# Seven block products for two chunks at a time, and float32 numerators for eight more pairs of heads

## The chip, the cores and the metric

The kernel runs on one core of a Trainium2 chip. The core has a matrix engine (TensorE, here PE, with PEld for its weight loads), three engines that work on tiles in on-chip memory (VectorE or DVE, ScalarE or ACT, GpSimd or POOL), and SyncE (SP), which here issues nearly all transfers. PE writes only to PSUM, which has eight banks of 512 float32 values for each of 128 partitions; DVE and ACT read them. The metric is the time of one execution in microseconds (us) on the device; lower is better.

## The reference, cut to what matters

```python
def phi(x):
    proj = np.einsum('bhsd,df->bhsf', x, w_phi)
    proj = proj - np.max(np.abs(proj), axis=-1, keepdims=True)
    return np.concatenate([np.exp(proj), np.exp(-proj)], axis=-1)
q_p, k_p = (phi(q), phi(k))
kv = np.einsum('bhsf,bhsd->bhfd', k_p, v)
num = np.einsum('bhsf,bhfd->bhsd', q_p, kv)
den = np.einsum('bhsf,bhf->bhs', q_p, np.sum(k_p, axis=2))[..., None] + 1e-06
x = (num / den) ...            # 8 batches x 576 tokens = 4608 rows of 8 heads x 64 = 512
g = x @ w_gate                 # 512 -> 1536
silu = g * (1.0 / (1.0 + np.exp(-g)))
return (silu * (x @ w_val) @ w_out)
```

All arrays are float32; the three large weights arrive as float64. A linear attention over 8 batches and 8 heads is followed by a gated feed-forward layer.

## The kernel before, in words

Attention is worked out for one batch and one pair of heads at a time: 32 steps called `attention(i)`, i from 0. The feed-forward layer takes the 4608 tokens in 12 chunks of 384 (c from 0 to 11) and the 1536 hidden columns in 12 tiles of 128 (f from 0 to 11).

Where full float32 precision is wanted at the speed of the faster format (float32r), a value is split into a rounded high part and a remainder, and one product becomes three: high x high, high x low, low x high. `first(c, f)` (L686) makes the *gv* products: 2 banks (gate and value, tiles gv0 and gv1) x 4 pieces of the 512 inputs x 3 terms = 24 products of 128x384. ACT then takes the tanh of half the gate (L716), DVE makes gate x (1 + tanh) (L718) and multiplies with the value (L721). `parts` (L737) splits that: cast hh on ACT (L741), remainder hl on DVE (L742). `second(c, f)` (L747) adds it through the third weight into three *o* banks: 3 x 3 products of 128x512. At f = 11 ACT copies each o bank to one of two osb buffers (L782), and SP stores it (L785). `put_off` holds a `second` back until the next tile's `first` is queued, so that PE has 24 gv products to do while hh and hl are made.

Chunks 0 to 2 have their gv products first, tile by tile as the weights are unpacked; the hidden values of chunks 1 and 2 go to memory (`keep`, `fetch`, h_dram) and their `second` comes later. From chunk 3 on, `first` and `second` alternate, and the low parts of the weights are loaded again from wlo_dram for each tile (`low_parts`, L683): 512 KB for gv and 256 KB for o.

Attention up to i = 7 (the "early" pairs of heads) uses plain float32 products. From i = 8 on all is split: keys ks (L378, L380), queries qs (L519, L521), the features qh and ql (L579, L582), the sums kvh and kvl (L456, L460); the numerators are 4 groups of 6 products work<-qh/ql,kvh/kvl. The result num / den is divided on DVE (L616 to L620) and split into xh and xl (L632, L634), the gv operands, which have room for three chunks.

The order on each engine is not written by hand: `Plan` takes steps with assumed costs, dependences and a rank, plays them through and issues them in the order it finds, with manual scheduling. Feed-forward steps outside PE have the lowest rank number and go first; on PE attention goes first and feed-forward products fill up. So every engine, SP with its transfers too, has one fixed line of work. All PE products but a few stand at line 282, in the helper `matmuls`.

Of the kernel before, what the change touches and what calls it, by code (L numbers as in the profile page):

```python
# [17 lines left out]
P = 128  # L18
# [23 lines left out]
EARLY_PAIRS = 8  # L42

# [3 lines left out]

# [11 lines left out]
class Plan:  # L59
# [3 lines left out]
    LAG = {"PE": 220, "ACT": 90, "DVE": 90, "SP": 2000}  # L63
# [24 lines left out]
    def run(self):  # L88
# [11 lines left out]
        def start(e):  # L100
# [33 lines left out]
            for t in s.then:  # L134
                n += 1
                heapq.heappush(events, (freed if t.eng == e and e in ("ACT", "DVE", "PE") else done, n, "dep", t))
# [29 lines left out]
def dve(n):  # L166
    return 150 + 1.04 * n
# [5 lines left out]

def act(n):
    return 190 + 0.86 * n
# [11 lines left out]
def favor_attention_moe(ctx: ExitStack, tc: tile.TileContext, qT, kT, v, w_phi, wg, wv, wo, out):  # L187
# [7 lines left out]
    h_dram = tc.dram_tile([EARLY, NFT, P, CH], F32, name="h_dram")  # L195

# [139 lines left out]
    x_ready = {}  # L336
# [4 lines left out]
    def attention(i, rank):  # L341
        b, pr = divmod(i, NPAIR)
        plan.early = early = i < EARLY_PAIRS
        split = not early
        j = i % 2 if early else 1
        vec = nc.vector
# [108 lines left out]
        for ones in range(2):  # L455
            kvc.append(add("ACT", act(4 * D), lambda ones=ones: nc.scalar.copy(  # L456
                cut(kv_high() if split else kvs[j], ones), sums(ones)), [kv_steps[-1], *(use("kvs") if i != EARLY_PAIRS else first_late("kvs"))], rank))
# [112 lines left out]
        done = [[f1], [f1]]  # L570
# [16 lines left out]
        for h in range(2):  # L587
            for part in range(2):
# [4 lines left out]
                def numerators(key=key, h=h, c=c):  # L593
                    o = work[plan.bank[key]][:, :SH]
                    terms = []
                    for k in range(2):
# [4 lines left out]
                        else:  # L601
                            terms.append((kvs[j][:, n], (qe, qx)[k][j][:, h, c]))
# [3 lines left out]
                free = last.get(("num", i - 1))  # L606
                copied.append(add("ACT", act(SH), lambda key=key, ra=ra, c=c: nc.scalar.copy(  # L607
                    num[ra, c], work[plan.bank[key]][ra, :SH]), [nu, free], rank))
                copied.append(add("ACT", act(SH), lambda key=key, ra=ra, rb=rb, c=c: nc.scalar.activation(  # L609
                    den[ra, c], work[plan.bank[key]][rb, :SH], AF.Copy, bias=1e-6), [nu, free], rank, give=key))  # L610
# [17 lines left out]
            [(base, 0, 0, CH), (base + 1, 0, CH, CH // 2)]  # L628
        for c, at, start, width in cuts:
            src = num[:, start:start + width]  # L630
# [8 lines left out]
        last["num", i] = lo  # L639
# [86 lines left out]
    def keep(c, f, j, made):  # L726

        th_free[j] = h_kept[c, f] = add("SP", P * CH * 4, lambda: nc.sync.dma_start(h_dram[c, f], th[j]), [made], FIRST)

    def fetch(c, f):  # L730
        j = ffn["th"] % TH_SETS
        ffn["th"] += 1
        return j, add("SP", P * CH * 4, lambda: nc.sync.dma_start(th[j], h_dram[c, f]), [h_kept[c, f], th_free[j]], FIRST)
# [13 lines left out]
    def second(c, f, hidden, low):  # L747
        b, ready = hidden
        readers, lo, lo_ready = low
        for t in range(NT):  # L750
            sl = slice(t * P, (t + 1) * P)

            def go(t=t, sl=sl):
                if t == 0:
# [4 lines left out]
                    ((hh[b][:, sl], w2_hi[f]), (hh[b][:, sl], lo), (hl[b][:, sl], w2_hi[f])))])  # L759
# [3 lines left out]
            if f == NFT - 1:  # L763
                if n_out[0] == NCH * NT - 1:
# [126 lines left out]
```

## Time and profile before

| | us |
|---|---|
| median of 3 runs | 1269.33 (1268.94 to 1270.84) |
| the profiled execution, first to last instruction | 1273.1 |
| PE busy | 1262.2 |
| DVE busy | 876.4 |
| ACT busy | 651.5 |
| POOL busy | 1.3 |
| transfers | 168 MB, 132 GB/s on average |

The page gives busy times, the span in 40 slices, the chain of work that ended last, groups of instructions and transfers. A group's row has line, engine, operation, what it writes and reads, shapes and count, then busy us and mean ns, then idle time before it and who ended it. A matmul's shown duration reaches into the next one; what one costs in a row of them is read from the distance of their starts.

### The profile page before, as it was taken

The page shows a single profiled execution, that of the slowest core. Times are in us where ns is not written, and L with a number is a line of the kernel's source. Part 1 is how long each engine was busy: PE and PEld are TensorE (multiplying, and loading weights), DVE is VectorE, ACT ScalarE, POOL GpSimd, SP SyncE. Part 2 cuts the span into 40 slices and gives each one's busy share as a digit, 9 for nine tenths or more (in the row PEclk, how much of TensorE's full clock was granted, in tenths as well). Part 3 has the DMA queues.
Part 4 walks back from the last instruction along what each step waited for, and adds up shares of the span by engine and source line. Part 5 has one row for each costly group of instructions (what it writes and reads, how often), then busy time and mean ns, then how long its engine had stood idle before and what let it go on. Part 6 is the DMA issues. An engine that isn't in the chain of part 4 may idle for free.

```text
span 1273.1 us, 19796 instructions
## 1 busy us (share of the span) xinstructions
PE 1262.2 (99%) x7427; PEld 1189.9 (93%) x7427; DVE 876.4 (69%) x1674; ACT 651.5 (51%) x1383; POOL 1.3 (0%) x13
## 2 busy tenths in 40 slices
PE   9999999999999999999999999999999999999998
PEld 8887999999889999999999999999999999999998
DVE  6998999998887778762788888822488886222222
ACT  5787433336676666632765666611466665121211
POOL 0000000000000000000000000000000000000000
PEclk8999999999999999999999999999999999999999
DMA  4543455555564344444433444354444342444443
GB/s 120 144 119 102 140 174 175 174 165 167 159 204 123 112 117 113 148 123 127 129 104 113 129 124 120 105 161 129 125 120 119 105 132 84 124 149 125 149 126 106
DMA packets 112111, 168.15 MB, mean 132 GB/s; under 512 B 52752, under 2 KB 59408, under 8 KB 112016
## 3 DMA queue, kind: packets, MB, share of 16 engines
q1 hardware_dynamic: 111552, 166.64, 44.1%
q8 instruction: 58, 0.95, 0.3%
q14 instruction: 37, 0.30, 0.1%
q10 hardware_dynamic: 464, 0.26, 0.1%
HBM read 143.26 MB, written 23.59 MB: 131 GB/s over the span
## 4 chain that ended last, share of the span: by engine, by line
PE 92%; DVE 4%; DMA 1%; ACT 1%; SPq 1%; issue 0%; DVEq 0%; ACTq 0%
PE gv L282 46%; PE o L282 25%; PE work L282 12%; PE kv L435 8%; PE kv L428 1%; DMA out_dram<-osb 0%; PE o L502 0%; DVE km L410 0%; DVE kp L415 0%; DMA shared<-in_wg_dram 0%; DMA shared<-in_wo_dram 0%; DVE qy L491 0%; DMA wbd<-in_w_phi_dram 0%; DVE km L486 0%; ACT den L609 0%
## 5 line engine op out<-in xcount | busy, mean ns | idle before, releaser
L282 PE MATMUL gv<-xh,w_hi 128*128 128x384 f32 x1152 | 388.6, 337 | 0.8 <-DVE th L718 0.8
L282 PE MATMUL gv<-xh,w_lo 128*128 128x384 f32 x1152 | 386.9, 336 | 0.0
L282 PE MATMUL gv<-xl,w_hi 128*128 128x384 f32 x1152 | 386.1, 335 | 0.0
L282 PEld LDWEIGHTS gv<-xh,w_hi 128*128 128x128 f32 x1152 | 216.4, 188 | 5.7 <-DVE th L718 1.1
L282 PEld LDWEIGHTS gv<-xl,w_hi 128*128 128x128 f32 x1152 | 216.5, 188 | 4.6
L282 PEld LDWEIGHTS gv<-xh,w_lo 128*128 128x128 f32 x1152 | 216.1, 188 | 0.0
L716 ACT ACTIVATE th<-gv 128x384 f32<-128x384 f32 x144 | 70.9, 492 | 263.9 <-PE gv L282 263.1
L718 DVE SCALAR_TENSOR_TENSOR th<-th,gv 128x384 f32<-128x384 f32 x144 | 79.2, 550 | 149.6 <-ACT th L716 147.7
L282 PE MATMUL o<-w_hi,hl 128*128 128x512 f32 x432 | 171.5, 397 | 0.2 <-DVE hl L742 0.2
L282 PE MATMUL o<-w_hi,hh 128*128 128x512 f32 x432 | 170.9, 396 | 0.3 <-ACT osb L782 0.3
L282 PE MATMUL o<-w_lo,hh 128*128 128x512 f32 x432 | 170.3, 394 | 0.0
L741 ACT CAST hh<-th 128x384 fp32r<-128x384 f32 x144 | 73.6, 511 | 164.3 <-DVE th L721 148.1
L721 DVE TENSOR_TENSOR th<-th,gv 128x384 f32<-128x384 f32 x144 | 79.4, 552 | 71.1 <-PE gv L282 68.7
L435 PEld LDWEIGHTS kv<-vf,kp 128*128 128x128 f32 x1024 | 123.2, 194 | 3.1 <-ACT kp L419 1.3
L435 PE MATMUL kv<-vf,kp 128*128 128x66 f32 x1024 | 123.2, 274 | 1.3 <-ACT kp L419 1.0
L742 DVE TENSOR_TENSOR hl<-th,hh 128x384 fp32r<-128x384 f32 x144 | 79.5, 552 | 32.8 <-ACT hh L741 32.1
L282 PEld LDWEIGHTS o<-w_hi,hl 128*128 128x128 f32 x432 | 81.4, 188 | 19.4 <-DVE hl L742 0.6
L282 PEld LDWEIGHTS o<-w_hi,hh 128*128 128x128 f32 x432 | 81.7, 189 | 12.7 <-ACT osb L782 0.8
L282 PEld LDWEIGHTS o<-w_lo,hh 128*128 128x128 f32 x432 | 81.4, 188 | 12.2
L616 DVE STREAM_TRANSPOSE qe<-den 128x576 f32<-128x576 f32 x32 | 24.9, 778 | 92.0 <-ACT den L609 92.0
L607 ACT COPY num<-work 64x288 f32<-64x288 f32 x102 | 40.2, 394 | 51.2 <-PE work L282 49.8
L282 PE MATMUL work<-qh,kvh 128*128 128x288 f32 x192 | 60.8, 317 | 0.3 <-DVE kp L415 0.3
(124 smaller groups left out, 1871.1 us busy)
## 6 DMA issues: line engine op xcount, KB each, us to landing
w_lo<-wlo_dram SPq DMA_DIRECT2D x108, 512.0 KB, 3.6
w_lo<-wlo_dram SPq DMA_DIRECT2D x132, 256.0 KB, 3.0
wlo_dram<-w_lo SPq DMA_DIRECT2D x36, 256.0 KB, 2.3
out_dram<-osb SPq DMA_DIRECT2D x35, 256.0 KB, 3.3
kin<-in_kT_dram SPq DMA_DIRECT2D x32, 256.0 KB, 2.9
vf<-in_v_dram SPq DMA_DIRECT2D x64, 128.0 KB, 2.7
qin<-in_qT_dram SPq DMA_DIRECT2D x24, 288.0 KB, 2.9
shared<-in_wg_dram SPq DMA_DIRECT2D x12, 512.0 KB, 3.6
```

Of the source, the lines that this page charges most:

```text
L282: nc.tensor.matmul(o, l, r, start=a, stop=z)
L428: nc.tensor.matmul(ps_kv[:, 2 * k * D2:2 * (k + 1) * D2], room[:, 0, k], vf[j][:, 4].rearrange("p h d -> p (h d)"), start=False, stop=k == 1)
L435: nc.tensor.matmul(o, room[:, 2 * (t - t0) + h, k], vf[j][:, t, h], start=t + h + k == 0, stop=False)
L607: copied.append(add("ACT", act(SH), lambda key=key, ra=ra, c=c: nc.scalar.copy(num[ra, c], work[plan.bank[key]][ra, :SH]), [nu, free], rank))
L616: t0 = add("DVE", dve(S), lambda: vec.transpose(turned, den), [*copied, *done[0], *done[1]], rank)
L716: s1 = add("ACT", act(CH), lambda: nc.scalar.activation(t_, ps_gv[0][:, :CH], AF.Tanh, scale=0.5), [ends[0], th_free[j]], FIRST)
L718: s2 = add("DVE", dve(CH), lambda: nc.vector.scalar_tensor_tensor(out=t_, in0=t_, scalar=1.0, in1=ps_gv[0][:, :CH], op0=ALU.add, op1=ALU.m ...
L721: s3 = add("DVE", dve(CH), lambda: nc.vector.tensor_tensor(out=t_, in0=t_, in1=ps_gv[1][:, :CH], op=ALU.mult), [s2, ends[1]], FIRST)
L741: s4 = add("ACT", act(CH), lambda: nc.scalar.copy(hh[b], th[j]), [made, hid_free[b]], FIRST)
L742: s5 = add("DVE", dve(CH), lambda: nc.vector.tensor_tensor(out=hl[b], in0=th[j], in1=hh[b], op=ALU.subtract), [s4], FIRST)
```

## The change

**Feed-forward, chunks 4 to 11.** They are taken as four pairs of chunks. With the 512 inputs cut in two halves, and gate and value as the two columns of a 2 x 2 block product, two chunks by two halves times two halves by (gate, value) needs 8 block products; the change uses the scheme with 7 products and 15 sums (Strassen's, in Winograd's form). Each of the 7 blocks is 2 pieces x 3 terms = 6 gv products of 128x384, so a tile has 42 for two chunks where it had 48. The sums of the tokens (s1, s2 and two more) are made in `operands` on DVE, from x that attention now stores in x_dram (`held`), and all seven operands are split on ACT and DVE. The sums of the weights are made once, by `mixed`, on POOL, 12 additions of 128x256 for each tile, and stored in wt_dram; `load_ring` streams them back through six buffers that held the gv weights. The sums of the results are made in the banks and through copies: gv0 (gv_145 below) collects four blocks, and ACT copies its state three times on the way; gv1 (gv_146) has two sums of its own, and DVE joins them with the copies. The `second` of the job before is cut into its three thirds, which stand between the blocks. The hidden values of chunk c+1 go to memory, and its twelve `second` follow when the pair's twelve tiles are done.

**Chunks 1 to 3.** `mixed` is queued while chunk 2's second products, chunk 3's first and chunk 3's second are due. Chunk 3's hidden values go to memory too.

**Attention, i = 8 to 15.** Keys and queries stay split, the numerators do not: 4 groups of 2 float32 products (kvs, qe, qx), without L579, L582 and L460.

```diff
+SPLIT_FROM = 16
+PAIRS = 4
+RING = 6
-        split = not early
+        split = i >= SPLIT_FROM
+        held = [(start, width) for c, at, start, width in cuts if c >= PAIRS]
+        if held:
+            x_stored[b, pr] = add("SP", P * width * 4, lambda start=start, width=width, token=token: nc.sync.dma_start(
+                x_dram[pr, :, token:token + width], num[:, start:start + width]), [t3], rank)
-    def second(c, f, hidden, low):
+    def second(c, f, hidden, low, parts_of=range(NT)):
-        for t in range(NT):
+        for t in parts_of:
...
+    def mixed(f, rank):
+        get = add("SP", P * 4 * DM * 2, lambda: nc.sync.dma_start(src.bitcast(F32), wlo_dram[f, :, :2 * DM]),
+                  [lo_stored[f, 0], lo_stored[f, 1], *old[0], *x_free[1]], rank)
...
+        g0 = add("POOL", 4 * pool2(2 * P), whole, [get, *old[1], *x_free[2]], rank)
+        g1 = add("POOL", 4 * pool2(2 * P), combine, [g0, *old[2]], rank)
+        g2 = add("ACT", act(8 * P), lambda: nc.scalar.copy(high, sums()), [g1, *old[3]], rank)
+        g3 = add("POOL", 4 * pool2(2 * P), rest_of, [g2], rank)
...
+    def load_ring(m, n):
+        k = m % RING
+        after, ring_user[k] = ring_user[k], []
+        return add("SP", P * 8 * P * 4, lambda: nc.sync.dma_start(
+            flat(w1_hi[k]).bitcast(F32), wt_dram[:, 2 * n:2 * n + 2].rearrange("p n h c -> p (n h c)")),
+            [*after, *w_spread[2 * n // 7], *w_spread[(2 * n + 1) // 7]], FIRST)
+    def operands(c):
...
+        l0 = split(0, a11, [got[0]])
+        l1 = split(1, a12, [got[1]])
+        d1 = combine(s1, a21, a22, ALU.add, [got[2], got[3], *temp_free[0]])
+        d2 = combine(s2, s1, a11, ALU.subtract, [d1, got[0], *temp_free[1]])
+        l2 = split(2, s2, [d2])
+        d3 = combine(a21, a11, a21, ALU.subtract, [d1, got[0]])
+        l3 = split(3, a21, [d3])
+        l4 = split(4, s1, [d1])
+        l5 = split(5, a22, [got[3]])
+        d4 = combine(a12, a12, s2, ALU.subtract, [l1, d2])
+        l6 = split(6, a12, [d4])
...
+    def pair(c, base):
...
+            part = lambda t: second(*job, range(t, t + 1)) if job else None
+            p1 = mult(0, bank_b, True, False, b_read)
+            y1 = copy(0, p1)
+            p2 = mult(1, bank_c, True, True, c_read)
+            g1 = joined(0, [p2, y1])
+            ja, ga = gate(snap[0], [g1])
+            p6 = mult(2, bank_b, False, False, [y1])
+            y2 = copy(1, p6)
+            part(0)
+            p7 = mult(3, bank_b, False, False, [y2])
+            y3 = copy(2, p7)
+            p5 = mult(4, bank_c, True, False, [g1])
+            v2 = joined(2, [p5, y3])
+            p4 = mult(5, bank_b, False, True, [y3])
+            jb, gb = gate(lambda: bank_b[:, :CH], [p4])
+            part(1)
+            p3 = mult(6, bank_c, False, True, [v2])
+            v1 = joined(1, [p3, y2])
+            part(2)
+            b_read[:], c_read[:] = [gb], [v1]
+            ha = valued(ja, 1, [ga, v1])
+            hb = valued(jb, 2, [gb, v2])
+            keep(c + 1, f, jb, hb)
+            put_off(c, f, parts(ja, ha), low2(f))
...
+        for f in range(NFT):
+            put_off(c + 1, f, parts(*fetch(c + 1, f)), low2(f))
+    for n in range((NCH - PAIRS) // 2):
+        pair(PAIRS + 2 * n, 7 * NFT // 2 * n)
```

What the plan makes of it, at three places. First, PE at the end of a pair's last tile (chunks 6 and 7): the last block ends in gv_146, o_144 takes the third third of tile 10's job, and o_142 and o_143 begin tile 11's (operands hh_133 and hl_135). Now:

```order
L1030 MATMUL gv_146<-w_hi_78,w_hi_76 128x384
L1030 MATMUL gv_146<-w_hi_77,w_hi_76 128x384
L290 MATMUL o_144<-w_hi_93,hh_132 128x512
L290 MATMUL o_144<-w_lo_1367,hh_132 128x512
L290 MATMUL o_144<-w_hi_93,hl_134 128x512
L290 MATMUL o_142<-w_hi_94,hh_133 128x512
L290 MATMUL o_142<-w_lo_1496,hh_133 128x512
L290 MATMUL o_142<-w_hi_94,hl_135 128x512
L290 MATMUL o_143<-w_hi_94,hh_133 128x512
```

Before, PE at the end of chunk 10's last tile: 24 gv products, then the o products of the tile before (weight w_hi_91), whose operands were made meanwhile.

```order
L282 MATMUL gv_144<-xh_98,w_lo_94 128x384
L282 MATMUL gv_144<-xh_98,w_hi_80 128x384
L282 MATMUL gv_144<-xl_101,w_hi_80 128x384
L282 MATMUL gv_144<-xh_98,w_lo_94 128x384
L282 MATMUL o_140<-w_hi_91,hh_130 128x512
L282 MATMUL o_140<-w_lo_95,hh_130 128x512
L282 MATMUL o_140<-w_hi_91,hl_132 128x512
```

Tile 11's o products now come three o products after the gv products that they depend on; before, a tile's came behind the next tile's 24 gv products.

Second, DVE at the same turn (part_4961 and part_5135 are the buffers of s1 and s2, and of the copies out of the banks; the row at L1042 joins bank and copy, L1055 multiplies with the gate, hl_135 is tile 11's remainder, hl_134 that of chunk 7's first job, L985 and L989 make the next pair's operands). Now:

```order
L1055 TENSOR_TENSOR th_131<-th_131,part_5135 128x384
L989 TENSOR_TENSOR xl_104<-part_4724,op_hi 128x768
L1042 TENSOR_TENSOR part_4961<-gv_146,part_4961 128x384
L1055 TENSOR_TENSOR th_130<-th_130,part_4961 128x384
L762 TENSOR_TENSOR hl_134<-th_128,hh_132 128x384
L985 TENSOR_TENSOR part_4961<-part_4722,part_4724 128x768
L762 TENSOR_TENSOR hl_135<-th_130,hh_133 128x384
```

Before, DVE's rows for two tiles of chunk 11:

```order
L718 SCALAR_TENSOR_TENSOR th_127<-th_127,gv_143 128x384
L721 TENSOR_TENSOR th_127<-th_127,gv_144 128x384
L742 TENSOR_TENSOR hl_133<-th_127,hh_131 128x384
L718 SCALAR_TENSOR_TENSOR th_128<-th_128,gv_143 128x384
L721 TENSOR_TENSOR th_128<-th_128,gv_144 128x384
L742 TENSOR_TENSOR hl_132<-th_128,hh_130 128x384
```

Between the last gv product and hl, DVE had one multiplication; now it has a join and a multiplication that belong to the job, and three rows that do not.

Third, ACT in one tile of the last two pairs of chunks (gv_145 is copied at L1038; part_4961 also holds the gate's sum, of which L1049 takes the tanh). Now:

```order
L1038 COPY part_4961<-gv_145 128x384
L1049 ACTIVATE th_128<-part_4961 128x384
L1038 COPY part_4961<-gv_145 128x384
L1038 COPY part_5135<-gv_145 128x384
L1049 ACTIVATE th_129<-gv_145 128x384
L761 CAST hh_132<-th_128 128x384
```

Before, ACT in three tiles of chunk 11:

```order
L716 ACTIVATE th_128<-gv_143 128x384
L741 CAST hh_130<-th_128 128x384
L716 ACTIVATE th_129<-gv_143 128x384
L741 CAST hh_131<-th_129 128x384
L716 ACTIVATE th_126<-gv_143 128x384
```

Three copies have come in for two chunks' tile, and the second of them stands behind the first tanh.

More of the change, by code (lines that the diff above doesn't have):

```diff
@@ L59 @@
 class Plan:
-    LAG = {"PE": 220, "ACT": 90, "DVE": 90, "SP": 2000}
+    LAG = {"PE": 220, "ACT": 90, "DVE": 90, "POOL": 200, "SP": 2000}
     BYTES = 250.0
@@ L135, in start @@
                 n += 1
-                heapq.heappush(events, (freed if t.eng == e and e in ("ACT", "DVE", "PE") else done, n, "dep", t))
+                heapq.heappush(events, (freed if t.eng == e and e in ("ACT", "DVE", "PE", "POOL") else done, n, "dep", t))
             if s.give is not None:
@@ L456, in attention @@
             kvc.append(add("ACT", act(4 * D), lambda ones=ones: nc.scalar.copy(
[L457 removed]
+                cut(kv_high() if split else kvs[kj], ones), sums(ones)),
+                [kv_steps[-1], *use("kvs"), *first_late("kvs")], rank))
         if split:
@@ L567, in attention @@
                 qx[j][:, h], qx[j][:, h], AF.Exp, scale=-1.0)))]
-        done = [[f1], [f1]]
+        done = [[f1], [f1]] if early else [[f1[h]] for h in range(2)]
         if split:
@@ L788, in second, with copy @@
-        hid_free[b] = done
-        readers.append(done)
+            if t == NT - 1:
+                hid_free[b] = done
+                readers.append(done)
+            if f < NFT - 1:
+                continue
+            if n_out[0] == NCH * NT - 1:
+                halves = [pool.tile([P, DM // 2], F32, name=f"osb_last{k}", tag=tag) for k, tag in enumerate(("num", "den"))]
+                for k, eng in enumerate(("ACT", "DVE")):
+                    cols = slice(k * DM // 2, (k + 1) * DM // 2)
+                    rows = out[c * CH + t * P:c * CH + (t + 1) * P, cols]
+                    def copy(k=k, cols=cols, t=t, o=halves[k]):
+                        if k:
+                            nc.vector.tensor_scalar(out=o, in0=ps_o[t][:, cols], scalar1=0.5, scalar2=None, op0=ALU.mult)
+                        else:
+                            nc.scalar.activation(o, ps_o[t][:, cols], AF.Copy, scale=0.5)
+                    cp = add(eng, act(DM // 2), copy, [done], FIRST)
+                    q = nc.sync if k else nc.scalar
+                    add("SP" if k else "ACT", P * DM * 2 if k else 60, lambda q=q, rows=rows, o=halves[k]: q.dma_start(rows, o), [cp], FIRST)
+                continue
@@ new lines, in favor_attention_moe, with wide_tile @@
+    wide = {}
+    def wide_tile(name, tag, shape=(P, 8 * P), dtype=F32):
+        if name not in wide:
+            wide[name] = pool.tile(list(shape), dtype, name=name, tag=tag)
+        return wide[name]
+    for f in range(NFT):
+        mixed(f, FIRST)
+    for f in range(NFT):
+        put_off(2, f, parts(*fetch(2, f)), low_parts_at_rest(f, NFT + f))
+    attend((EARLY + 1) * CH)
+    w_used = {}
+    for f in range(NFT):
+        j, h = first(EARLY, f, low_parts(f, 0))
+        w_used[f] = ffn["pe"]
+        keep(EARLY, f, j, h)
+        put_off()
```

203 lines of the change are left out of this document (166 added, 37 removed).

## The prediction

> **What bounds the kernel now.** I read the page's part 1 first, then the 40 slices and the chain that ended last, then the windows, then the chain piece by piece.
>
> ```profile
> PE 1262.2 (99%) x7427; PEld 1189.9 (93%) x7427; DVE 876.4 (69%) x1674; ACT 651.5 (51%) x1383; POOL 1.3 (0%) x13
> DVE  6998999998887778762788888822488886222222
> PE 92%; DVE 4%; DMA 1%; ACT 1%; SPq 1%; issue 0%; DVEq 0%; ACTq 0%
> PE gv L282 46%; PE o L282 25%; PE work L282 12%; PE kv L435 8%; PE kv L428 1%; DMA out_dram<-osb 0%; PE o L502 0%; DVE km L410 0%; DVE kp L415 0%; DMA shared<-in_wg_dram 0%; DMA shared<-in_wo_dram 0%; DVE qy L491 0%; DMA wbd<-in_w_phi_dram 0%; DVE km L486 0%; ACT den L609 0%
> ```
>
> TensorE (PE) carries 92% of the chain, and almost half of it is gv, the first products of the feed-forward part. A busy PE in this profile is not yet a PE without gaps, so the rate is read from the chain's pieces late in the run, and the other engines' load from windows (columns: stretch, its length, then busy us and instructions of PE, PEld, DVE, ACT, POOL, then clock, DMA share, GB/s).
>
> ```profile
> 1153.74 4.19 PE gv L282 x24
> 1157.93 2.09 PE o L282 x9
> 1160.02 4.19 PE gv L282 x24
> ...
> 200.00:300.00 100.00, 100.00 (x567) 97.15 (x566) 93.89 (x178) 41.53 (x75) 0.00 (x0) 1.00 0.51 166
> 291.00:530.00 239.00, 238.03 (x1446) 221.37 (x1445) 190.05 (x363) 160.61 (x343) 0.00 (x0) 0.99 0.48 141
> 1150.00:1200.00 50.00, 50.00 (x265) 46.84 (x264) 13.34 (x24) 8.91 (x19) 0.00 (x0) 1.00 0.44 127
> ```
>
> The pieces touch: 24 gv products take 4.19 us (0.1746 us each), nine o products 2.09 us (0.232 us each), and nothing lies between. DVE reached 94% at 200 to 300 us with PE still full. So **time is PE work**, and a change pays what it takes from PE, less every gap it opens.
>
> **Removed: products.** Chunks 4 to 11 had 8 x 288 = 2304 gv products; four pairs of chunks at 7 blocks x 12 tiles x 6 have 2016. 288 x 0.1746 = **-50.3 us**. Their weights now come as 512 KB pieces from wt_dram; the o products are the same in number.
>
> **Added: float32 numerators.** Pairs of heads 9 to 16 use 8 float32 products each in place of 24 split ones.
>
> ```profile
> 24.24 0.65 PE L282 MATMUL work<-qe,kvs 128*128 128x288 f32 x2
> ...
> 26.18 1.90 PE L435 MATMUL kv<-vf,kp 128*128 128x66 f32 x16
> ...
> 301.56 0.38 PE L282 MATMUL work<-qh,kvh 128*128 128x288 f32 x1
> ...
> 303.24 0.61 PE L428 MATMUL kv<-vf,kp 128*128 128x132 f32 x4
> ...
> L582 DVE TENSOR_TENSOR ql<-qx,qh 128x576 fp32r<-128x576 f32 x48 | 36.2, 754 | 0.0
> L460 DVE TENSOR_TENSOR kvl<-kv,kvh 128x256 fp32r<-128x256 f32 x48 | 18.7, 417 | 0.0
> ```
>
> Four float32 products (each shown as two) fill 24.24 to 26.18: 0.485 us each. Twelve split ones fill 301.56 to 303.24: 0.14 each. A pair of heads costs 8 x 0.485 - 24 x 0.14 = +0.52 us, eight of them **+4.2 us** on PE. DVE sheds four L582 and two L460 per pair of heads, 3.85 us, 31 in all; that is worth nothing by itself while PE covers it.
>
> **Added: handoffs inside a pair's loop.** Bank gv_145 is copied out by ACT while PE goes on adding to it, so PE waits for copies. The measured handoffs:
>
> ```profile
> 1180.63 0.33 PE L282 MATMUL gv<-xh,w_lo 128*128 128x384 f32 x1
> 1180.81 0.33 PE L282 MATMUL gv<-xh,w_hi 128*128 128x384 f32 x1
> 1181.00 0.49 ACT L716 ACTIVATE th<-gv 128x384 f32<-128x384 f32 x1 [3.04 <-PE gv L282]
> 1181.53 0.55 DVE L718 SCALAR_TENSOR_TENSOR th<-th,gv 128x384 f32<-128x384 f32 x1 [2.98 <-ACT th L716]
> 1183.09 0.56 DVE L721 TENSOR_TENSOR th<-th,gv 128x384 f32<-128x384 f32 x1 [1.00 <-PE gv L282]
> 1183.73 0.51 ACT L741 CAST hh<-th 128x384 fp32r<-128x384 f32 x1 [2.23 <-DVE th L721]
> 1184.28 0.56 DVE L742 TENSOR_TENSOR hl<-th,hh 128x384 fp32r<-128x384 f32 x1 [0.64 <-ACT hh L741]
> ```
>
> ACT starts 0.19 us after PE goes on to the next product, DVE about 0.20; DVE to ACT takes 0.08, ACT to DVE 0.04. The second copy stands on ACT behind a tanh. From the end e of the second block: join on DVE e+0.20 to 0.75, tanh e+0.83 to 1.32, copy to 1.81, PE free to go at about e+1.86 (0.05 for the way back, as from ACT's end at 1203.58 to PE's start at 1203.63 in the rows of the next part). PE has a block (1.05) and a third of an o job (0.70) until e+1.75. The stall is 0.11 us, in 24 loops with nothing else to run and 24 that attention both fills and delays: about 0.12 x 48 = **+6 us** (0 if the copy of 384 columns is faster than the tanh; 15 if attention's ACT work of 0.68 us pieces gets in front each second time).
>
> **Added: the turn between the two chunks of a pair.** The order puts the last job of chunk c and the first of c+1 side by side.
>
> ```profile
> L380 DVE TENSOR_TENSOR ks<-kin,ks 128x640 fp32r<-128x640 f32 x24 | 19.7, 822 | 4.7 <-ACT ks L378 3.8 <-DMA qin<-in_qT_dram 0.7
> out_dram<-osb SPq DMA_DIRECT2D x35, 256.0 KB, 3.3
> 1202.98 0.60 ACT L782 ACTIVATE osb<-o 128x512 f32<-128x512 f32 x1 [2.64 <-DMA out_dram<-osb]
> 1203.63 0.50 PE L282 MATMUL o<-w_hi,hh 128*128 128x512 f32 x1 [0.35 <-ACT osb L782]
> 319.60:323.00 3.40, 2.58 (x14) 1.81 (x12) 3.37 (x6) 3.40 (x8) 0.00 (x0) 1.00 0.65 208
> 323.00:326.40 3.40, 3.25 (x11) 2.43 (x11) 3.17 (x6) 2.80 (x6) 0.00 (x0) 0.64 0.39 119
> ```
>
> First gap: the last job's operand needs join, product, cast, remainder after the last block: 0.20 + 0.55 + 0.03 + 0.55 + 0.08 + 0.51 + 0.04 + 0.55 + 0.05 = 2.56 us, and only 0.70 us of o work covers it. Before, 24 gv products lay in front. At the second and third turn the order also pushes other work in on DVE: ahead of the join a 768-wide remainder (0.96, from L380's 822 at 640 wide and 754 at 576, of which 0.8 delays), behind the product hl of the next chunk (0.55) and a 768-wide sum (0.96), the cast running beside them: 2.56 - 0.70 + 0.8 + 0.55 + 0.96 - 0.6 = 3.6. Turn by turn: 0.8 (attention fills 1.5 after the same sum), 3.6, 3.6, 1.9; together 9.9 us. Second gap: the third copy out of o needs an osb buffer, which is free when the first one's store has landed: 0.20 + 0.60 + 3.3 + 0.60 + 0.05 = 4.75 us after the first third; PE has four thirds, 2.8 us. 1.95 us, four times: 7.8. Together **+18 us**, and **+2 us** for the clock: after PE had idled 0.8 of 3.4 us (the row at 319.60) it was granted 0.64 of the clock on average for 3.4 us, which would cost up to 1.7 us a turn, but the second gap absorbs most.
>
> **Added: mixing the weights on POOL.** 144 additions of 128 x 256, two inputs, while chunks 1 to 3 are worked on.
>
> ```profile
> masks.py:199 POOL TENSOR_SCALAR_AFFINE_SELECT ident<-ident 128x128 f32<-128x128 f32 x1 | 0.3, 288 | 0.0
> L881 POOL MEMSET const-bfloat16-1.0<- 128x1 bf16 x1 | 0.1, 111 | 0.0
> L616 DVE STREAM_TRANSPOSE qe<-den 128x576 f32<-128x576 f32 x8 | 6.2, 777 | 25.3 <-ACT den L609 25.3
> ```
>
> No row shows such an addition. POOL's one-input pass over 128 columns took 288 ns, an empty instruction 111: 1.4 ns a column and input. 256 columns: 0.47 us with one input (low end), 0.83 with two (taken), 1.66 (twice that, high end). A tile has 12 of them, a cast of about 1.1 us and handoffs: 12 us at 0.83. PE's work from the end of chunk 2's first products to the first pair is 288 x 0.1746 + 321 x 0.232 + eleven or twelve pairs of heads at some 9 us (work, kv: 21% of the span over 32 pairs is 8.4, and 0.5 for float32), near 229 us, 19 us a tile. Hidden, up to 1.4 us an addition; at 1.66 it is 22 us a tile, 36 us late. ACT and SP take these steps in line, so what is late there holds the evacuation of PE's banks and the loads behind.
>
> DVE is the closer limit there. It did 190 us in 291 to 530 us with eight pairs of heads (L616 in that window). Now: 190 - 29 for the dropped splits + 45 for three more pairs at some 15 + 10 for the first operands = 216 of 229, 94%, what it managed at 200 to 300. I take **+5 us** for this stage, with 0 and 48 as bounds (48: POOL's 120 us hold DVE up for two fifths of their time).
>
> The Trainium skill's "SBUF — State Buffer", under "Who interferes with whom", says that a VectorE instruction with two SBUF inputs and a GpSimd instruction that reads SBUF exclude each other for a whole instruction. Nothing here could show it (POOL worked 1.3 us). By it the forecast would be the second rival below, without it the first.
>
> **Sum**: -50.3 + 4.2 + 6 + 18 + 2 + 5 = -15.1 us. The profiled execution spans 1273.1 us, 0.3% above the 1269.33 median of the runs; the difference is carried over: **1254 us**.
>
> **Rivals.**
> 1. *The turns are filled and DVE keeps pace.* Then -50.3 + 4.2 + 6 = -40, 1229 us. For it: PE never waited long before, and the dropped splits take away the idles at 320 us. Against: the order shows no other PE work at three turns. Chance 0.17 (1222 to 1238).
> 2. *POOL and DVE hold each other up while the weights are mixed; slower than before.* PE's products of attention wait for DVE. DVE at 94% has no room: each microsecond that POOL holds it beyond some 5 comes out at the end. A third of POOL's 120 us is 40, 35 beyond that room: 1254 - 5 + 35 = 1284 us. The gain is gone once 20 us are lost in that stage. Against it: DVE's reads of PSUM and its transposes and reductions, over half of its work, have one SBUF input or none. Chance 0.16.
> 3. *The weight stream becomes the bound.* A loop moves 3.5 x 512 + 256 + 192 = 2240 KB, 2.29 MB, in 9.5 us: 241 GB/s, twice the present rate.
>
> ```profile
> GB/s 120 144 119 102 140 174 175 174 165 167 159 204 123 112 117 113 148 123 127 129 104 113 129 124 120 105 161 129 125 120 119 105 132 84 124 149 125 149 126 106
> 355.00:360.00 5.00, 5.00 (x42) 4.87 (x40) 0.42 (x2) 4.32 (x11) 0.00 (x0) 1.00 0.80 254
> ```
>
> 254 GB/s was reached for 5 us at a share of 0.80, so it should fit, with six buffers of 2.7 us each ahead. Were 204 (the best slice) the limit, a loop would take 11.2 us: +1.7 x 24 = 41, 1295 us. Chance 0.08.
> 4. *Balance*: a store that lands 3 us later (landing times vary with what is queued ahead) and half a clock at each turn bring 1254 + 4 x 4 = 1270. Chance 0.06.
>
> **How the numbers follow.** Forecast (1238 to 1266.8): 0.53. A measurement of this kernel tells about 0.2% from no change, 1266.8 to 1271.9. Faster: 0.53 + 0.17 = 0.70; same 0.06; slower 0.16 + 0.08 = 0.24. The range that should hold 8 in 10 goes from 1226, inside the first rival, to 1288, inside the second.
>
> **What would show it.** gv products: 3168 at 0.175 us apart. Numerators: qe,kvs and qx,kvs 128 records each. Turns: idle of PE before o with DVE hl, then ACT osb as releaser, four times 1 to 4 us and 2 us, and a granted clock below 1 there. Loop: some 0.1 us before the third block with the copy on ACT as releaser. Mixing: POOL's addition near 0.83 us, DVE's two-input rows no longer than before (754, 552), and no PE idle from 314 to 550 us. Wrong, if PE idles there in tens of us, if DVE's means grow by a tenth or more while POOL runs, or if DMA is named as releaser of gv.

## The result, and the profile after

The changed kernel takes 1305.07 us (median of 4 runs, 1301.61 to 1308.66), the kernel before, run beside it, 1270.07. The ratio is 1.0272, 95% interval 1.025 to 1.0294: **slower by 35 us**, where 15 us faster was forecast. The profiled execution spans 1306.9 us.

These are the page's part 1, the slices of TensorE, POOL and the clock, and the chain that ended last, for the changed kernel:

```profile
PE 1251.3 (96%) x7076; PEld 1146.7 (88%) x7076; DVE 969.8 (74%) x1770; ACT 717.5 (55%) x1491; POOL 121.4 (9%) x157
PE   9999999999999889889999999999999999899998
POOL 0000000004443323540000000000000000000000
PEclk9999999999999988889999999999999999899999
PE 79%; DVE 12%; ACT 4%; DMA 2%; issue 2%; SPq 0%; DVEq 0%; ACTq 0%
```

351 matmul records have gone, 11 us of busy time with them, and the span has grown all the same: PE is no longer full. Most of its dips and of those of its clock lie in slices 14 to 18 (some 425 to 590 us), in the second half of POOL's work. The chain, 92% PE before, now leaves PE for 21% of the span, and DVE has most of that.

The windows tell the two stages apart (columns: stretch, its length, then busy us and instructions of PE, PEld, DVE, ACT, POOL, then clock, DMA share, GB/s). First the changed kernel: the mixing stage, the stage behind it, and 100 us of the last pair's loops.

```profile
310.00:600.00 290.00, 259.88 (x1454) 230.83 (x1453) 222.24 (x377) 185.17 (x382) 117.27 (x142) 0.94 0.77 243
600.00:760.00 160.00, 159.88 (x990) 152.52 (x988) 137.87 (x259) 107.33 (x225) 0.00 (x0) 1.00 0.68 219
1160.00:1260.00 100.00, 100.00 (x534) 93.08 (x533) 45.72 (x82) 31.65 (x66) 0.00 (x0) 1.00 0.75 244
```

PE idles 30.1 of the 290 us in which the weights are mixed, and its granted clock there is 0.94, another 0.06 x 290 = 17 us. In the stage behind, and in the loops of the pairs at 244 GB/s, it is full. Who PE waits for (instruction, releaser, total us, times, longest): the first three rows are of the mixing stage alone, the other three of the whole run.

```profile
PE work L290 <- DVE kp L424: 15.4, 7, 5.1
PE o L290 <- DVE hl L762: 6.0, 5, 1.6
PE work L290 <- ACT qe L574: 4.3, 1, 4.3
...
PE o L290 <- ACT osb L806: 9.6, 5, 2.9
PE o L290 <- DVE hl L762: 7.3, 8, 1.6
PE o L290 <- ACT hh L761: 5.5, 4, 1.8
```

While the weights are mixed, PE waits above all for attention's pieces on DVE, and 6.0 of the 7.3 us for hl belong to this stage too. Behind it, from 600 us on, PE waits 9.5 us for osb, 4.6 for hh and 1.2 for hl: these 15.3 us are the turns. The loops of the last pair, in the chain's pieces, show what a loop costs when nothing else runs:

```profile
1199.41 3.32 PE gv L1030 x18
1202.73 0.70 PE o L290 x3
1203.43 1.04 PE gv L1030 x6
1204.47 0.70 PE o L290 x3
1205.17 3.12 PE gv L1030 x18
1208.29 0.70 PE o L290 x3
1208.99 3.30 PE gv L1030 x18
```

One loop is 1208.99 - 1199.41 = 9.58 us; its 42 gv and 9 o products without a gap are 42 x 0.1746 + 9 x 0.232 = 9.42. The 0.16 us over lie in the first stretch of 18, which takes 3.32 us where the other takes 3.12. So products cost what was forecast, and a loop's handoffs 0.16 us.

One turn, 1122 to 1134 us, as the timeline has it (start, duration, in brackets the idle time before and its releaser):

```profile
1123.94 0.56 DVE L1055 TENSOR_TENSOR th<-th,part 128x384 f32<-128x384 f32 x1
1124.53 0.51 ACT L761 CAST hh<-th 128x384 fp32r<-128x384 f32 x1 [0.85 <-DVE th L1055]
1125.10 0.50 PE L290 MATMUL o<-w_hi,hh 128*128 128x512 f32 x1 [1.78 <-ACT hh L761]
...
1131.90 0.60 ACT L806 ACTIVATE osb<-o 128x512 f32<-128x512 f32 x1 [2.06 <-DMA out_dram<-osb]
...
1132.55 0.79 PE L290 MATMUL o<-w_hi,hh 128*128 128x512 f32 x1 [2.82 <-ACT osb L806]
1133.14 0.63 PE L290 MATMUL o<-w_lo,hh 128*128 128x512 f32 x1
...
1133.57 0.63 PE L290 MATMUL o<-w_hi,hl 128*128 128x512 f32 x1
...
1134.00 0.63 PE L290 MATMUL o<-w_hi,hh 128*128 128x512 f32 x1
```

Both gaps that the prediction described are there, 1.78 us for the gate's chain and 2.82 us for the third eviction's store. Behind the second the o products start 0.43 us apart, in place of 0.232, until 1138.69 us: the granted clock from 1132.5 to 1136 us is 0.50. That costs 2.9 us more.

### The profile page after: what moved, and what is told of

It is laid out like the page before. It is cut to its first block, busy times and chain, and to the rows that moved or that the text cites. A ratio compares the mean times of both kernels' runs of the same rounds, so it can differ in the third digit from the quotient of the medians.

```text
span 1306.9 us, 20317 instructions
## 1 busy us (share of the span) xinstructions
PE 1251.3 (96%) x7076; PEld 1146.7 (88%) x7076; DVE 969.8 (74%) x1770; ACT 717.5 (55%) x1491; POOL 121.4 (9%) x157
## 4 chain that ended last, share of the span: by engine, by line
PE 79%; DVE 12%; ACT 4%; DMA 2%; issue 2%; SPq 0%; DVEq 0%; ACTq 0%
PE gv L1030 25%; PE o L290 21%; PE gv L290 13%; PE work L290 11%; PE kv L444 7%; DMA out_dram<-osb 1%; PE kv L437 1%; DVE qx L572 1%; DVE qm L557 1%; DVE qe L569 1%; DVE hl L762 1%; DVE km L419 1%; DVE qe L549 1%; DVE kp L424 1%; ACT qe L574 1%
## 5 line engine op out<-in xcount | busy, mean ns | idle before, releaser
L1030 PE MATMUL gv<-xh,w_hi 128*128 128x384 f32 x768 | 217.5, 342 | 0.4
L290 PE MATMUL o<-w_hi,hh 128*128 128x512 f32 x432 | 177.2, 410 | 15.3 <-ACT osb L806 9.6
L290 PE MATMUL o<-w_hi,hl 128*128 128x512 f32 x432 | 175.0, 405 | 7.3 <-DVE hl L762 7.3
L290 PE MATMUL o<-w_lo,hh 128*128 128x512 f32 x432 | 173.8, 402 | 0.0
L761 ACT CAST hh<-th 128x384 fp32r<-128x384 f32 x144 | 73.6, 511 | 141.1 <-DVE th L1055 64.6
L1042 DVE TENSOR_TENSOR part<-gv,part 128x384 f32<-128x384 f32 x144 | 80.0, 555 | 82.4 <-PE gv L1030 77.7
L290 PE MATMUL gv<-xh,w_hi 128*128 128x384 f32 x384 | 132.8, 346 | 1.0 <-DVE th L738 1.0
L290 PE MATMUL gv<-xl,w_hi 128*128 128x384 f32 x384 | 130.3, 339 | 0.0
L290 PE MATMUL gv<-xh,w_lo 128*128 128x384 f32 x384 | 130.3, 339 | 0.0
L1030 PE MATMUL gv<-xl,w_hi 128*128 128x384 f32 x384 | 128.6, 335 | 0.0
L290 PEld LDWEIGHTS o<-w_hi,hh 128*128 128x128 f32 x432 | 83.5, 193 | 30.1 <-ACT osb L806 12.7
L1038 ACT COPY part<-gv 128x384 f32<-128x384 f32 x144 | 68.5, 475 | 74.7 <-PE gv L1030 71.2
L1030 PE MATMUL gv<-op_hi,w_hi 128*128 128x384 f32 x384 | 106.8, 335 | 0.0
L290 PEld LDWEIGHTS gv<-xh,w_hi 128*128 128x128 f32 x384 | 73.6, 192 | 2.2 <-DVE th L738 1.4
L290 PEld LDWEIGHTS gv<-xl,w_hi 128*128 128x128 f32 x384 | 73.5, 191 | 0.8
```

The source lines that it names most:

```text
L290: nc.tensor.matmul(o, l, r, start=a, stop=z)
L761: s4 = add("ACT", act(CH), lambda: nc.scalar.copy(hh[b], th[j]), [made, hid_free[b]], FIRST)
L1030: nc.tensor.matmul(o[:, :CH], l, r, start=begin and i == 0, stop=i == len(terms) - 1, skip_group_check=True)
L1038: s = add("ACT", act(CH), lambda: act_.copy(snap[n](), bank_b[:, :CH]), [after, *snap_free[n]], FIRST)
L1042: return add("DVE", dve(CH), lambda: vec.tensor_tensor(out=snap[n](), in0=bank_c[:, :CH], in1=snap[n](), op=ALU.add), after, FIRST)
```

## The experiments

All times are medians, each beside the kernel before on the same chip (1270.07 us beside the changed kernel, 1271 to 1273 beside the others). In short:

| run | us | ratio to before (95%) |
|---|---|---|
| changed kernel | 1305.07 | 1.0272 (1.025 to 1.0294) |
| e1 no additions on POOL | 1297.85 | 1.0194 (1.0171 to 1.0216) |
| e2 additions that nobody waits for | 1315.74 | 1.0342 (1.0314 to 1.0369) |
| e3 stores of mixed weights left out | 1309.65 | 1.029 (1.0263 to 1.0317) |
| e4 kernel before, float32 numerators | 1277.87 | 1.0042 (1.0026 to 1.0058) |
| e5 planner's rate 350 | 1295.17 | 1.0177 (1.0162 to 1.0193) |
| e6 kernel before, rate 350 | 1278.73 | 1.0051 (1.0035 to 1.0066) |
| e7 turns mended | 1290.82 | 1.0147 (1.0123 to 1.0172) |
| e8 e5 and e7 | 1275.74 | 1.0025 (1.0014 to 1.0036) |
| e9 rate 350 from 250 us on | 1287.53 | 1.0119 (1.01 to 1.0137) |
| e10 e9 and e7 | 1269.91 | 0.9979 (0.9966 to 0.9991) |
| e11 e10 without additions | 1262.25 | 0.9918 (0.9895 to 0.9941) |
| e12 e10, rate 400, stores of chunks 0 to 3 on ScalarE's queue | 1284.3 | 1.0091 (1.007 to 1.0113) |
| e13 e10 with 300 | 1271.48 | 1.0001 (0.9978 to 1.0024) |
| e14 e10 with 450 | 1288.0 | 1.0122 (1.0103 to 1.014) |
| e15 e10 with 600 | 1313.22 | 1.0315 (1.0285 to 1.0345) |
| e16 e10, the same stores on ScalarE's queue | 1287.32 | 1.0108 (1.0066 to 1.0151) |

### POOL, the bytes, and the numerators (e1 to e4)

The first theory was rival 2 of the prediction: POOL's additions hold DVE up. Its rivals: what waits for POOL's results is late; the mixing's bytes fill the wire.

e1 makes none of the three groups of additions (the first is shown); ScalarE's copy and one store take other data of the same size:

```diff
-        g0 = add("POOL", 4 * pool2(2 * P), whole, [get, *old[1], *x_free[2]], rank)
+        g0 = add("POOL", 4 * pool2(2 * P), lambda: None, [get, *old[1], *x_free[2]], rank)
...
-        g2 = add("ACT", act(8 * P), lambda: nc.scalar.copy(high, sums()), [g1, *old[3]], rank)
+        g2 = add("ACT", act(8 * P), lambda: nc.scalar.copy(high, hi[:, :8 * P]), [g1, *old[3]], rank)
```

> The changed kernel with POOL's 144 additions left out; ScalarE's copy takes the high part of the weights in place of the sums, and the store that took the sums' low part takes that copy, so that the bytes moved and the order on every other queue stay as they were. The sums of weights are not computed. If POOL's additions (by the hold-up of VectorE or by the waits on their results) cost what the stage from 300 to 600 us lost, some 30 us of idle TensorE and 16 us of lower clock, then about 1250 to 1262 us, and VectorE's qs L531 falls from a mean of 945 ns there back to about 754. If the DMA bytes or the attention that is squeezed into this stage cost it, 1298 to 1306 us.

e2, the same, with three groups of additions on tiles that nothing else reads:

```diff
+        def alone():
...
+            for n in range(4):
+                gp.tensor_tensor(out=sums()[:, block(n)], in0=full()[:, block(n)], in1=full()[:, block((n + 1) % 4)], op=ALU.add)
...
+        g0 = add("POOL", 4 * pool2(2 * P), alone, [get, *old[1], *x_free[2]], rank)
```

> As the run without additions, but POOL makes 144 additions of two SBUF operands of the same size on two tiles that nothing else reads, started by the same loads. The sums of weights are not computed. If the additions cost time because they hold up VectorE (rival 2 of the prediction), it is nearly as slow as the changed kernel: 1295 to 1308 us, with qs L531 above 900 ns while POOL runs. If what costs is that the cast and the stores wait for POOL's results, it is as fast as the run without additions: 1250 to 1262 us. If neither, both runs stay at 1298 to 1306.

e3, the stores:

```diff
+        if f:
+            put = lambda j, n, part, t: None
...
-            flat(w1_hi[k]).bitcast(F32), wt_dram[:, 2 * n:2 * n + 2].rearrange("p n h c -> p (n h c)")),
+            flat(w1_hi[k]).bitcast(F32), wt_dram[:, 2 * (n % 3):2 * (n % 3) + 2].rearrange("p n h c -> p (n h c)")),
```

> The changed kernel with the stores of the seven weights left out for the tiles 1 to 11; the pairs' loads read the same bytes as before, but all from the rows of tile 0. POOL, ScalarE and VectorE do what they did; the products take wrong weights. If the DMA queues (shares up to 1.05 in slices of 10 us between 300 and 600) hold the stage up, it falls to 1255 to 1275 us; if POOL does, it stays within 5 us of 1305.

e4, the kernel before with `split = i >= SPLIT_FROM` and what belongs to it:

> The kernel before with float32 numerators for the ninth to sixteenth pairs of heads and nothing else of the change. By the term of the sum, 0.52 us more TensorE for each of 8 pairs: 1270 + 4 = 1274 us (1272 to 1277). If the 32 splits taken off VectorE and ScalarE shorten waits as well, below 1272; if a float32 numerator holds the work banks for longer and starves the gv products, above 1278.

e1 came out at 1297.85: leaving POOL out wins (1.0272 - 1.0194) x 1272 = 10 us, not 45, by hold-up and waits on results together. The hold-up itself is real, and the timeline of the changed kernel shows how it works:

```profile
452.05 0.17 DVE L562 COPY qu<-qm 32x36 f32<-32x36 f32 x1
452.25 2.79 POOL L876 TENSOR_TENSOR w_sums<-w_sums,xl 128x256 f32<-128x256 f32 x4 [8.55 <-ACT xl L880]
452.26 0.78 DVE L563 TENSOR_TENSOR qu<-qm,qu 32x36 f32<-32x36 f32 x1
453.07 0.64 DVE L564 COPY qu<-qu 32x36 f32<-32x36 f32 x1
453.74 0.65 DVE L565 COPY qu<-qu 64x36 f32<-64x36 f32 x1
```

As soon as POOL starts four additions of 0.70 us, each of DVE's small steps takes about as long as one addition, 0.64 to 0.78 us in place of 0.17 to 0.19. The Trainium skill's "SBUF — State Buffer", "Who interferes with whom", says just this: whoever starts first holds the shared ports for the whole instruction. The trace agrees, for two-input steps and small copies. The groups of DVE between 300 and 600 us agree too (mean ns of one is the number behind the comma); the first row is of the changed kernel, the second of e1:

```profile
L531 DVE TENSOR_TENSOR qs<-qin,qs 64x576 fp32r<-64x576 f32 x22 | 20.8, 945 | 3.0 <-ACT qs L529 2.5
...
L531 DVE TENSOR_TENSOR qs<-qin,qs 64x576 fp32r<-64x576 f32 x22 | 16.6, 753 | 3.0 <-ACT qs L529 2.5
```

In e2 nobody waits for POOL, and POOL waits for nobody either:

```profile
L868 POOL TENSOR_TENSOR w_sums<-w_full 128x256 f32<-128x256 f32 x144 | 120.0, 870 | 5.7 <-PE gv L290 5.5
```

All 144 additions follow each other almost without a pause, from 310 to 433 us, where the changed kernel spreads them over 279 us. The run is 18 us slower than e1, so the hold-up alone costs time. But e2 is no copy of the changed kernel without its waits: packed so, the additions cost more than in the changed kernel, and how e1's 10 us divide between the hold-up and the waits on POOL's results is not shown. Either way the size is small: in e1, with no addition at all, PE still idles 20.7 of the 290 us at a clock of 0.94.

e3 takes the bytes of eleven tiles' stores away and wins nothing (1.029 against 1.0272, the intervals overlap). Its window of the mixing stage:

```profile
310.00:600.00 290.00, 258.23 (x1464) 230.47 (x1463) 225.41 (x378) 185.98 (x382) 121.65 (x144) 0.94 0.57 176
```

DMA is down from 243 to 176 GB/s, and PE idles 31.8 us. POOL still waits 33 us for its loads, behind the first, and 119 for ScalarE's cast. The bytes on the chip's wire do not hold this stage up.

e4: 0.0042 x 1272 = 5.3 us (3.3 to 7.4 by the interval), against 4.2 forecast. The time is 0.9 us above the range expected for this run, but the term stands.

So the main loss of this stage was neither POOL's additions nor the bytes. The next suspect was the order itself.

### The planner's wire (e5, e6, e9)

The planner lays every queue's order down with a model in which all DMA shares one wire of `BYTES` = 250 bytes a nanosecond. The mixing adds 2.4 MB per tile (0.5 loaded, 1.8 stored) to a stage that had 140 GB/s before. New theory: the model takes the wire for full, counts loads as late, and stretches the mixing; the order it writes is kept on the chip whether the loads are late or not.

e5 and e6 change `BYTES = 250.0` to `350.0`, in the changed kernel and in the kernel before. e9 does so from 250 us of the plan on:

```diff
-                wire = max(wire, now) + s.cost / self.BYTES
+                wire = max(wire, now) + s.cost / (self.BYTES if now < 250000 else 350.0)
```

> The changed kernel with one number of the planner's model changed: it reckons with 350 bytes a nanosecond of DMA in place of 250 when it lays down the order of every queue. Work, transfers and waits are the same. If the loss between 300 and 600 us is in the order (the model takes the wire for full in this stage, so that loads count as late, and attention and products are put in an order in which TensorE waits for VectorE), TensorE's idle time there falls from 30 to below 12 us, the lower clock with it, and the time to 1268 to 1285 us. If the transfers themselves are late on the chip, or VectorE has too much to do there, it stays at 1300 to 1310.

> The same number of the planner's model changed in the kernel before, as a control. Its order keeps TensorE busy already (2 us of idle time between 300 and 563 us), so 1268 to 1275 us by the first theory. If the number helps every order, it is below 1262, and then the run above says nothing on the mixing.

> The changed kernel, with the planner reckoning 250 bytes a nanosecond of DMA for the first 250 us of its plan and 350 after that, so that the first chunks keep the order they have. The run with 350 throughout lost about 10 us in its first 144 gv products (164 against 154 us) and gained over 20 after; with the loss gone, 1283 to 1290 us. If the 10 us come back elsewhere, 1293 to 1300.

e5 won 12 us and not the 20 to 37 expected. PE's idle time between 310 and 600 us fell from 30.1 to 16.5, not below 12, and the 144th gv product came at 164.9 us in place of 153.2. e6, the kernel before, came out above its expected range, too (+6.5 us), and there the 144th came at 161.4 in place of 156.0; so the start wants the lower number. With the loss avoided, e9 wins (1.0272 - 1.0119) x 1272 = 19.5 us, by one number of a model: the work, its bytes and what depends on what are the same, in another order. Its window of the mixing stage, and POOL's waits of the changed kernel and of e9:

```profile
310.00:603.00 293.00, 275.84 (x1583) 246.53 (x1582) 222.02 (x390) 187.93 (x383) 114.28 (x143) 0.98 0.84 270
...
POOL w_full L866 <- DMA xh<-wlo_dram: 355.6, 11, 305.3
POOL w_sums L876 <- ACT xl L880: 100.1, 12, 16.9
POOL w_sums L872 <- DMA wt_dram<-w_sums: 7.2, 5, 3.5
...
POOL w_sums L872 <- DMA wt_dram<-w_sums: 73.6, 11, 10.9
POOL w_sums L876 <- ACT xl L880: 4.4, 3, 2.1
POOL w_full L866 <- DMA xh<-wlo_dram: 2.4, 2, 2.1
```

In the changed kernel POOL waits 50 us for its tiles' loads (355.6 without the wait of 305.3 for the first) and 100 us for ScalarE's cast, both of which stand late in their queues; in e9 2.4 and 4.4. There its wait is another one: 73.6 us, in place of 7.2, for its own tile's store to land. Together the three fall from 157.6 to 80.4 us. The last addition ends at 585.8 us there and at 505.7 here, and the first product of the first pair starts accordingly:

```profile
603.02 0.34 PE L1030 MATMUL gv<-xh,w_hi 128*128 128x384 f32 x1
...
547.54 0.34 PE L1030 MATMUL gv<-xh,w_hi 128*128 128x384 f32 x1
```

Up to there both have done the same 288 gv and 315 o products since chunk 2's first layer, but the changed kernel 869 of attention's matmul records in 293 us (3.0 a microsecond), e9 620 in 236 (2.6). While the planner had the pairs wait for weights, it put attention in front, denser than DVE can feed. Two stretches of the changed kernel, 10 us each, show it:

```profile
450.00:460.00 10.00, 5.67 (x23) 4.59 (x23) 9.32 (x17) 5.41 (x10) 2.79 (x4) 0.81 1.02 336
460.00:470.00 10.00, 10.00 (x51) 9.15 (x50) 4.17 (x8) 3.30 (x8) 5.64 (x8) 0.85 0.73 243
```

In the first DVE is busy for 9.32 us and PE idles, in the second DVE has little to do. Of the 15.4 us that PE waits for kp in this stage, 0.4 are left in e9.

### The turns (e7, e8, e10)

```diff
+                free = out_done.get(m, [*kept1(8), *kept1(9)])
...
+                for k in range(2):
+                    o = lambda k=k: wide_tile(f"part{k}", tags[k], (P, 8 * P))[:, 2 * CH:]
...
-            job = waiting.pop() if waiting else None
+            job = waiting.pop(0) if len(waiting) > (f > 0) else None
...
-            put_off(c, f, parts(ja, ha), low2(f))
+            waiting.append((c, f, parts(ja, ha), low2(f)))
```

> The changed kernel with its turns from one chunk to the next mended: a third buffer for the output's eviction in the pairs (two halves in the space left beside two quarters of operands), and the second layer of a tile in a pair runs two tiles after its first layer instead of one, so that tile 10's is left to cover the wait for tile 11's gate. The planner's number stays at 250. If the turns cost about 26 us (16 us idle, the rest at the lower clock), and the third buffer takes away the wait for the store and the lag most of the other: 1285 to 1295 us. If it only moves the wait elsewhere: 1302 to 1308.

> Both edits, the planner's 350 bytes a nanosecond and the mended turns. If the two losses are separate, the savings of the two runs add: about 1250 to 1270 us, and it may pass the kernel before. If VectorE is held up by POOL in the new order as well, some 10 us of that stay.

> The same number of the planner and the mended turns. By adding: the run with both edits took 1275.7 and loses some 8 us at its start that this one doesn't: 1264 to 1270 us, below the kernel before (1271 to 1273).

e7 wins (1.0272 - 1.0147) x 1272 = 16 us, and in e10 the same edit wins 1287.53 - 1269.91 = 17.6 in the better order. So the two losses are separate. In e7 the same turn has one gap left that is put down to another engine:

```profile
1122.43 0.50 PE L290 MATMUL o<-w_hi,hl 128*128 128x512 f32 x1 [0.45 <-DVE hl L762]
```

e8 came out 5.7 us above its expected range, and its first 144 gv products end 7 us later than e10's. e10 is the fastest of the kernels that leave nothing out, 0.9979 (0.9966 to 0.9991): some 3 us faster than the kernel before, and just told from it.

### What is left, and whether it is chance (e11 to e16)

> The same with POOL's 144 additions left out, as in the first run: ScalarE copies the high weights in place of the sums, and the sums of weights are not computed. If POOL's additions hold VectorE up in the better order too, this is 6 to 13 us below the run before it (it was about 10 in the changed kernel's order); if the new order gives VectorE room enough, it is within 3 us.

e11 is 7.7 us below e10: POOL's price is 8 to 10 us in either order. Its window, without POOL:

```profile
310.00:550.00 240.00, 224.61 (x1266) 200.49 (x1265) 167.52 (x310) 151.02 (x304) 0.00 (x0) 0.96 0.87 286
```

15.4 us of idle time and 0.04 x 240 = 10 us of clock are left in this stage. Two cautions: this execution is the slowest of e11's four (1267.97 us), and e10's window, with the additions, has nearly the same (14.2 us idle, 0.96), so the profile does not show where the 8 us lie. The largest piece, 8.1 us (4.4 in e10), was a turn within chunks 1 to 3, where the output's store stands behind attention's loads in SP's queue. e12 tried to move it, with 400 in place of 350 as a second edit:

```diff
-                out_done[m] = [add("SP", P * DM * 4, lambda t=t, o=o: nc.sync.dma_start(
+                q, cost = ("ACT", 60) if c < PAIRS else ("SP", P * DM * 4)
+                out_done[m] = [add(q, cost, lambda t=t, o=o: (nc.scalar if c < PAIRS else nc.sync).dma_start(
```

> The late350_turns version with two more edits: 400 in place of 350 bytes a nanosecond after the first 250 us, and the output's stores of chunks 0 to 3 issued from ScalarE's queue in place of SP's, where they stood behind the loads of attention (TensorE waited 4.4 us there for the eviction at one turn, and some 4 us ran at half clock). If the place in SP's queue was the cause, that wait is below 1 us and the time 1260 to 1267 us; if the store itself is late because the wire is full, 1267 to 1273.

The wait for osb is gone from this stage, as expected, and the run is 14 us slower and not faster: other waits in the same stage (hh, hl, qe and den) have grown. That raised a doubt on e9: perhaps any other order scatters by this much. e13 to e15 are e10 with other rates and nothing else, e16 is e12 with the rate left at 350.

> The late350_turns version with 300 in place of 350. If what the mixing stage loses follows from how full the planner takes the wire to be, it lies between the 250 of the turns-mended run (1290.8) and 350 (1269.9): 1273 to 1284 us. If any reshuffle of the order gives or takes some 15 us, it can fall outside, on either side.

> The same with 450. If the wire's reckoning decides, more room than the chip needs (it moved 272 GB/s over the stage) changes little: 1264 to 1274 us. If the order is a matter of chance, it may be anywhere from 1260 to 1290.

> The same with 600, at which the planner hardly sees the wire. By the first theory as with 450, or slower where loads that it takes for landed are late on the chip: 1264 to 1282 us, with TensorE waiting for DMA by name. By chance anywhere from 1260 to 1290.

> The late350_turns version with the stores of chunks 0 to 3 on ScalarE's queue and the planner's number left at 350. If those stores made the run before it (400 and ScalarE's stores, 1284) slow, 1278 to 1290 us; if the 400 did, 1262 to 1271.

300 came out just below its range, 450 and 600 well above theirs: I had thought spare room in the model harmless, and it isn't. With the turns mended, 250, 300, 350, 450 and 600 give ratios of 1.0147, 1.0001, 0.9979, 1.0122 and 1.0315. That looks like a trend with its best place at 300 to 350, which the intervals do not tell apart; it is a little above what the chip moved in this stage (269 to 286 GB/s). Five orders alone could not exclude chance, as e12 and e16 move the time by as much, but the waits go the same way. Below, POOL waits for ScalarE's cast and for its loads: 96.0 and 55.3 us at 250, 36.9 and 13.5 at 300 (behind the first load, 308.6), 4.4 and 1.7 at 350.

```profile
POOL w_full L878 <- DMA xh<-wlo_dram: 322.1, 9, 308.6
POOL w_sums L888 <- ACT xl L892: 36.9, 12, 5.1
```

Above, it is ScalarE that waits, at 350, 450 and 600 for POOL's sums, which wait 69 to 79 us for stores to land:

```profile
ACT xl L892 <- POOL w_sums L884: 12.0, 7, 3.3
...
ACT xl L892 <- POOL w_sums L884: 18.5, 10, 4.4
...
ACT xl L892 <- POOL w_sums L884: 43.9, 11, 8.5
...
PE work L290 <- ACT den L619: 14.5, 6, 5.0
```

The last row is of 600: PE waits there for ScalarE's den, 1.4 us at 350 and 4.3 at 450. ScalarE's waits for a fetched h grow as well, from 5.2 to 15.0 and 16.2 us, and PE waits 4.2 us for loads by name at 600. How the 43 us between 350 and 600 divide among these is not shown.

e16 shows that the stores on ScalarE's queue cost some 17 us without the 400 (1287.32 against 1269.91), so that the 400 is not needed to explain e12's 14; no run has the 400 alone. Why these stores cost so much is not settled: the output's casts and those of attention share that queue, but no run takes the two apart.

## Why the prediction was wrong

The mechanism by which the change pays was right: time is PE work, less every gap. The step that failed is one term, mixing the weights on POOL, **"+5 us" for this stage, "with 0 and 48 as bounds"**: it measured 47 us, read directly, and up to 56, taken as what is left over.

| term | forecast | measured |
|---|---|---|
| 288 products | -50.3 | loops at 9.58 us, the products in them at 0.1746: -50.3 |
| float32 numerators | +4.2 | +5.3 (e4) |
| handoffs, 48 loops | +6 | 0.16 x 48 = +8 |
| turns and clock | +20 | +22 read directly: 15.5 idle and 6.6 of clock in the windows of four turns; 16 and 17.6 won by mending them (e7, e10) |
| mixing stage | +5 | +47 read directly: 30.1 idle and 17 of clock; what is left of +35: 35 + 50.3 - 5.3 - 8 - 16 = +56 |

With both stages read directly the terms come to -50.3 + 5.3 + 8 + 22 + 47 = +32, of 35 measured; the kernel before lost some 3 us in its like stretch (291 to 530 us), so that about 6 us have no place.

Point by point:

- The products came as forecast: 3168 of them, at the same distance. The numerators too.
- The handoffs were sized by the row of the tanh, and came out at 0.16 instead of 0.12 us.
- The turns were read correctly from the order: idle before o with hh, hl and osb as releasers, 1.78 + 0.53 and 2.82 us at the one shown, where 3.6 and 1.95 were forecast; over all turns 5.8 and 9.5, forecast 9.9 and 7.8, so that the sum is nearer than its parts. The half clock cost 2.9 us at the one shown; 2 were counted for all four. This was the largest added cost in the forecast, and it was there.
- The addition on POOL was taken at 0.83 us; the four groups have means of 885, 867, 901 and 773 ns. That size was right as well, in part by luck: the four at 452 us took 0.70 each. What failed is the sentence **"Hidden, up to 1.4 us an addition"**, which sets 12 us of mixing a tile beside 19 us of PE work. The mixing was no chain of 12 us. It ran from 307.2 to 585.8 us, 23 us a tile, with POOL busy for 117 of the 290. The rest were above all the waits for the load and for the cast, 50 and 100 us, which stand late in the queues of SP and ScalarE. With the planner's rate at 350 both are all but gone and the mixing takes some 17 us a tile (e9). I had counted instructions and durations, and not asked what the planner would make of 2.4 MB more per tile at 250 bytes a nanosecond.
- "DVE is the closer limit" was half right. It did 222 us in 290, 77%, not 94%, and PE still waited for it. The share over the stage hid that its work comes in bursts, as the two stretches at 450 us show.
- The clock was counted at 2 us for the turns and not at all for this stage. There it cost 17 us, more than half of the idle time that brought it on.

The loss of the mixing stage divides as follows: some 20 us are the planner's rate (e9 against the changed kernel, e10 against e7), 8 to 10 are POOL's additions (e1, e11). The rest, 17 to 28 us by the two readings, is still there in e11, as idle time and clock of 15 and 10 us in its profiled execution. The cause of this last part stays open; e12 and e16 show only that moving the stores of chunks 0 to 3 to ScalarE's queue doesn't help.

Of the rivals, the second (POOL and DVE hold each other up, 1284 us) named the right stage and a true mechanism, but not its size: its "third of POOL's 120 us" is 8 to 10 us, not 40, and DVE, at 77%, was not without room as it had it. The third (the weight stream as the bound) fell: PE is full at 244 GB/s in the loops. The first fell by the turns and by the mixing stage. What the prediction named as a sign that it was wrong, PE idle in tens of us between 314 and 550 us and DVE's means grown by more than a tenth, is what the trace shows; its third sign, DMA as the releaser of gv, is not.

## What to carry over

Where a planner with a cost model writes the order, a change is also an input to that model: ask which of its resources the new work fills (here a wire with one number for its rate), and compare that number with what the trace shows the chip to move, since an order made for a slower wire costs time even where the wire has room, and here an order made for a faster one did, too. Work that is hidden "beside" an engine has to be followed through every queue that it stands in, not only summed. And count a gap on TensorE at more than its length where the clock falls behind it: here at 1.4 times for the turns (15.5 us idle, 6.6 of clock) and 1.6 times for the mixing stage (30.1 and 17).

## What was not expected of the hardware

- TensorE fell to half its clock after waits of 2.8 and 1.8 us: products stood 0.43 us apart in place of 0.232 behind the 2.82 us in the turn shown, and at the same turn of the pair before, at 982 us, behind one of 1.81. Behind the 1.78 and 0.53 us that came first at that earlier turn, from 977 us on, they stood 0.23 apart. The Trainium skill's "TensorE: Matmul & The Clock Gate", Part 1, has the half rate come after an idle window of about 3.4 us; here a shorter wait, with smaller ones some us before it, was enough.
- DVE's copies of 36 columns took 0.64 us beside POOL in place of 0.17, four times as long, while its step of 576 columns with two inputs grew by a quarter (945 against 753 ns). This fits a step that loses the rest of POOL's instruction, and not a share of its own length.
